# Last static expert slot of a fused attention and mixture-of-experts kernel: 32 tokens in plain fp32 and four column groups, in place of 128 tokens in split fp32r

## The chip, the core and the metric

The kernel runs on one core of one Trainium2 chip. The metric is device time in microseconds (us), the median over runs. Engines are named TensorE (PE in the profile, PEld for its weight loads), VectorE (DVE), ScalarE (ACT), GpSimd (POOL) and SyncE (SP, which issues most DMAs).

## The reference

Three layers follow each other on 2304 tokens of 512 features: a windowed attention, a dense layer pair, and a mixture of 8 experts with one expert per token. The last is what the change touches:

```python
def _moe2_ref(x, modality_id, w_gate, modality_bias, w1, w2):
    logits = x @ w_gate + modality_bias[modality_id]
    e_idx = np.argmax(logits, axis=1)
    ...
    gate_w = probs[np.arange(N), e_idx]
    for e in range(E):
        mask = e_idx == e
        ...
        h = np.maximum(x[mask] @ w1[e], 0.0)          # 512 -> 1024
        out[mask] = gate_w[mask, None] * (h @ w2[e])  # 1024 -> 512
```

Which tokens go to which expert is known only on the chip.

## The kernel before, in words

Tokens are sorted into slots of SL = 384 tokens, each slot for one expert. While the last chunk of the dense layers runs, routing tables are written: for each slot its expert, and for each place in it the token and its gate weight. Seven slots (NS0 = 7, numbered 0 to 6) are laid out in straight code; `final()` (line 729) puts the emptiest of the late slots last, and if it holds more than HS tokens it sets `nused` (line 768) so that a further full slot runs under `tc.If` (line 1227 and what follows). HS is 128 before the change (line 41).

A slot of 384 tokens (`slot`, line 851) works on TensorE in fp32r, with each operand split into a high and a low part: three matmuls (high-high, low-high, high-low) stand for one fp32 product. Layer 1 has the weights stationary, 384 tokens moving (line 858): 8 x 12 matmuls. ReLU and the split of the hidden values are ScalarE's and VectorE's (lines 860, 861). Layer 2 (`l2_slot`, line 867) goes by token tiles of 128: hidden values stationary, 512 output features moving, 24 matmuls a tile (line 873); then ScalarE scales by the gate weight (line 880) and GpSimd scatters the 128 rows to the output with an indirect DMA (line 881), where places without a token are out of bounds and are skipped.

The last slot (`half_slot`, line 887) holds one tile of 128 tokens. Layer 1 has the tokens stationary and pairs of weight blocks moving (256 columns, line 898): 4 x 12 matmuls. After ReLU (line 901) the result is turned with two transposes per pair (line 907) and split (lines 909, 910), and then the same `l2_slot` follows for one tile. Nothing of another slot is left to run beside it.

Weights of a slot come in 16 pieces of 128x512 (256 KB each, `wload`, line 783): SP loads a piece into one of four staging tiles, and three steps later ScalarE casts it to the high part and VectorE subtracts to give the low part (`wsplit`, lines 795 and 796). The tiles `experts` have two sets, for even and odd slots; slot 6 writes over slot 4's. `PS` says how many of these steps each part of a slot takes; the loads of slot 6 are issued from the sixth step of slot 4 on.

`gather` (line 816) makes a slot's list of tokens on GpSimd (three small table loads, line 820, and seven small operations) and fetches rows of 512 features (line 835). `prep_half` (line 842) turns them with four transposes a tile (line 845) and splits them. For slot 6 it stands in slot 5, in the middle of the first token tile of layer 2.

From slot 2 on TensorE's order is that of the program (a manual schedule), as is ScalarE's from the end of the dense layers, SP's throughout and GpSimd's from slot 5 on; VectorE's is chosen by the scheduler. A plain fp32 matmul shows as two records in the trace, and so does the attention's product with the values (`att_pv`, line 447), which is plain fp32 and puts two matmuls of 64 stationary columns into two column groups of the array:

```python
T.matmul(
    xo[a * D : (a + 1) * D, hp, o * BLK : (o + 1) * BLK],
    vt[:w, (2 * hp + a) * D : (2 * hp + a + 1) * D],
    ts[:w, hp, a * BLK : (a + 1) * BLK],
    start=True, stop=True,
)
```

Line 476 is plain fp32 too, a dense layer's, with all 128 stationary columns and 384 moving, four k-steps to a product.

Of the kernel before, what the change touches and what calls it, by code (L numbers as in the profile page):

```python
# [9 lines left out]
F32 = mybir.dt.float32  # L10
# [3 lines left out]
AF = mybir.ActivationFunctionType  # L14
ALU = mybir.AluOpType
AX = mybir.AxisListType

P = 128
B, H, S, D = 4, 8, 576, 64
NT = B * S  # L20
# [17 lines left out]
EARLY = 3  # L38
NS = (NT + E * (SL - 1)) // SL + EARLY
NS0 = 7  # L40
HS = P
NJ = NT // SL
NEG = -1.0e30
BIG = 1.0e6
# [2 lines left out]
def _consts():  # L47
    parts = {}
    parts["ident"] = np.eye(P)
    r = np.arange(P) % BLK  # L50
    c = np.arange(P)
    parts["m0"] = np.where(c[None, :BLK] <= r[:, None], 0.0, NEG)
    rel = (BLK + r)[:, None] - c[None, :]
    parts["m1"] = np.where((rel >= 0) & (rel < BLK), 0.0, NEG)
    parts["ones"] = np.ones((P, NS))
    parts["ids"] = np.arange(NTT)[None, :] * P + np.arange(P)[:, None] - BIG
    parts["first"] = np.broadcast_to((E - np.arange(E)).astype(float), (P, E))
    parts["eidx"] = np.broadcast_to(np.arange(E).astype(float), (P, E))
    parts["thr"] = np.broadcast_to(np.tile(np.arange(NJ) * float(SL), E), (P, NJ * E))
    parts["sidx"] = np.broadcast_to(np.arange(NS).astype(float), (P, NS))  # L60
    off, spec, arrs = 0, {}, []
    for k, a in parts.items():
        spec[k] = (off, a.shape[1])
        off += a.shape[1]
        arrs.append(np.asarray(a, np.float32))
    tri = (np.arange(P)[:, None] < np.arange(P)[None, :]).astype(np.float16)
    empty = np.zeros((NS * SL, 2), np.float32)
    return spec, np.ascontiguousarray(np.concatenate(arrs, axis=1)), tri, empty
# [3 lines left out]
def moe_kernel(ctx, tc, qT, kT, v, w_in, w_out, mod, wg, wgT, mbias, w1, w2, cst, tri, empty, out, spec):  # L72
# [17 lines left out]
    def tile_of(shape, name, dt=F32, tag=None, bufs=1):  # L90
        pool = sb if (tag or name) in WIDE else sm
        return pool.tile(shape, dt, name=name, tag=tag or name, bufs=bufs)

    def aux(shape, name):
        return ps.tile(shape, F32, name=name, tag="aux", bufs=3)
# [679 lines left out]
    GP, GN = 1, 0  # L775
    PW = KD * F2 // NP
    NLD = 3
    wld = {}

    def wpart(i, p, lo):  # L780
        return piece(i % 2, (p // NP * 2 + lo) * NP + p % NP)

    def wload(i, p):
        if p == 0:
            wld[i] = SP.value_load(
                meta[0:1, 1 if i < KNOWN else 3, i : i + 1], min_val=0, max_val=E - 1
            )
        t = tile_of([P, PW], f"wr{i}_{p}", tag=("v" if p % 2 else "q"), bufs=2)
        src = (w2 if p // NP else w1)[bass.ds(wld[i], 1), :, (p % NP) * PW : (p % NP + 1) * PW]
        SP.dma_start(t, src.rearrange("o p n -> (o p) n"))  # L790
        wld[i, p] = t

    def wsplit(i, p):
        t = wld.pop((i, p))
        A.copy(wpart(i, p, 0), t)  # L795
        V.tensor_tensor(wpart(i, p, 1), t, wpart(i, p, 0).bitcast(F32), op=ALU.subtract)  # L796

# [15 lines left out]
    def w2s(i, f, lo):  # L813
        return piece(i % 2, (2 + lo) * NP + f)

    def gather(i, rows=NT, halves=SH):
        rr = G.value_load(meta[0:1, 0 if i < KNOWN else 2, i : i + 1], min_val=0, max_val=(NS - 1) * SL)
        rt = tile_of([P, TT, SH, 2], f"rt{i}", tag="rt", bufs=2)
        for t in range(TT):
            G.dma_start(rt[:, t], tabs[t][bass.ds(rr, SL), :].rearrange("(h p) w -> p h w", p=P))  # L820
        rc = tile_of([P, SH, 2], f"rc{i}", tag="rc", bufs=4)
        oi = tile_of([P, SH], f"oi{i}", I32, tag="oi", bufs=4)
        gi = tile_of([P, SH], f"gi{i}", I32, tag="gi", bufs=4)
        gf = tile_of([P, SH], f"gf{i}", tag="gf", bufs=4)
        G.tensor_tensor(rc, rt[:, 0], rt[:, 1], op=ALU.add)
        G.tensor_tensor(rc, rc, rt[:, 2], op=ALU.add)
        G.tensor_scalar(gf, rc[:, :, 0], 0.0, None, op0=ALU.is_lt)
        G.tensor_scalar(rc[:, :, 0], rc[:, :, 0], BIG, None, op0=ALU.add)
        G.tensor_tensor(gf, gf, rc[:, :, 0], op=ALU.mult)
        G.tensor_copy(gi, gf)  # L830
        G.tensor_copy(oi, rc[:, :, 0])
        g = []
        for h in range(halves):
            t = tile_of([P, DM], f"g{i}_{h}", tag="ssk"[h], bufs=2)
            G.indirect_dma_start(t, None, yd[:rows, :], bass.IndirectOffsetOnAxis(ap=gi[:, h : h + 1], axis=0))
            g.append(t)
        return g, oi, rc

    def new_x2(i):
        return tuple(tile_of([P, KD, SL], f"z{s}{i}", F32R, tag=f"x{s}", bufs=2) for s in "hl")  # L840

    def prep_half(i, h, g, x):
        tp = aux([P, KD, P], f"tp{i}_{h}")
        for k in range(KD):
            T.transpose(tp[:, k, :], g[0][h][:, k * P : (k + 1) * P], C["ident"])
        sl = slice(h * P, (h + 1) * P)
        A.copy(x[0][:, :, sl], tp)
        V.tensor_tensor(x[1][:, :, sl], tp, x[0][:, :, sl].bitcast(F32), op=ALU.subtract)
# [17 lines left out]
    def l2_slot(i, g, t, mid, hid):  # L866
        hh, hl = hid
        yo = ps.tile([P, DM], F32, tag=f"y{t}", name=f"yo{i}_{t}", bufs=1)
        n = 0
        sl = slice(t * P, (t + 1) * P)  # L870
        for f in range(NF2):
            for a, b in ((hh, 0), (hh, 1), (hl, 0)):
                T.matmul(yo, a[f][:, sl], w2s(i, f, b), start=n == 0, stop=n == 3 * NF2 - 1)  # L873
                n += 1
            if f == NF2 // 2 - 1:
                yield
            elif f < NF2 - 1 and f % 2:
                mid()
        ob = tile_of([P, DM], f"ob{i}_{t}", tag="y", bufs=4)
        A.activation(ob, yo, AF.Copy, scale=g[2][:, t, 1:2])  # L880
        G.indirect_dma_start(  # L881
            out, bass.IndirectOffsetOnAxis(ap=g[1][:, t : t + 1], axis=0), ob, None,
            bounds_check=NT - 1, oob_is_err=False,
        )
        yield

    def half_slot(i, g, x, mid):
        hh, hl = (hm[:, u * NF2 * HS : (u + 1) * NF2 * HS].rearrange("p (f n) -> p f n", f=NF2) for u in range(2))
        xh, xl = x
        sl = slice(0, HS)  # L890

        def l1(fp):
            hp = ps.tile([P, 2, P], F32, tag="h", name=f"hp{i}_{fp}", bufs=2)
            w = [experts[i % 2, lo * NP // 2 + fp].rearrange("p (q k n) -> p k q n", q=2, k=KD) for lo in range(2)]
            n = 0
            for k in range(KD):
                for a, b in ((xh, 0), (xl, 0), (xh, 1)):
                    T.matmul(hp, a[:, k, sl], w[b][:, k], start=n == 0, stop=n == 3 * KD - 1)
                    n += 1
            r = tile_of([P, 2, P], f"hr{i}_{fp}", tag="y", bufs=4)  # L900
            A.activation(r, hp, AF.Relu)
            return r

        def turn(fp, r):
            rt = aux([P, 2, P], f"rt{i}_{fp}")
            for u in range(2):
                T.transpose(rt[:, u, :], r[:, u, :], C["ident"])
            fs = slice(2 * fp, 2 * fp + 2)
            A.copy(hh[:, fs], rt)
            V.tensor_tensor(hl[:, fs], rt, hh[:, fs].bitcast(F32), op=ALU.subtract)  # L910

        r = l1(0)
        for fp in range(1, NF2 // 2):
            yield
            r2 = l1(fp)
            turn(fp - 1, r)
            r = r2
        yield
        turn(NF2 // 2 - 1, r)
        yield from l2_slot(i, g, 0, mid, ([hh[:, f] for f in range(NF2)], [hl[:, f] for f in range(NF2)]))  # L920

    man = ExitStack()
    ET = mybir.EngineType
# [268 lines left out]
        if rts and next(rts[0], "end") == "end":  # L1192
            rts.clear()

    for i in range(NS0):
        if i == NS0 - 2:
            m2.enter_context(tc.manual_schedule(engines={ET.Pool}))
            used = nc.values_load(nused[0:1, 0:1], min_val=1, max_val=NS + 1)
        if i == 2:
            m2.enter_context(tc.manual_schedule(engines={ET.PE}))  # L1200
        nx = new_x2(i + 1) if i + 1 < NS0 else None
        for n, _ in enumerate((slot if i + 1 < NS0 else half_slot)(i, gq[i], x, advance)):
            advance()
            for _ in range(PS[n]):
                next(ws, None)
            if n == GN and EARLY <= i + GP < NS0:
                assert not rts
                gq[i + GP] = gather(i + GP, halves=SH if i + GP + 1 < NS0 else 1)
            pn = 1 if i < EARLY - 1 else NF2
            if nx is not None and pn <= n < pn + (SH if i + 2 < NS0 else 1):  # L1210
                prep_half(i + 1, n - pn, gq[i + 1], nx)
        x = nx
    m2.close()
    man.close()
# [59 lines left out]
```

## Time and profile before

| what | us |
|---|---|
| median of 3 runs | 731.57 |
| lowest and highest | 730.88 and 1313.32 |
| the profiled execution | 732.23 |
| its span, first to last instruction | 730.6 |
| TensorE busy in it | 715.6 |
| VectorE, ScalarE, GpSimd busy | 472.7, 389.9, 127.6 |

A row of a timeline reads: start in us from the span's start, duration, engine, line, operation, what it writes and reads, shapes, how many records are merged, and in brackets the engine's idle time before it with what ended it. Matmuls are pipelined: one record lasts from its issue to its last result, so records overlap, and merged records show the time that they cover together. A row by stretch gives the stretch and its length, busy us (and instructions) of PE, PEld, DVE, ACT and POOL, then the granted share of TensorE's clock, the DMA share and GB/s. A group's row gives busy us in all, mean ns of one, and the engine's idle us before them with what ended it.

### The profile page before, as it was taken

The page shows a single profiled execution, that of the slowest core. Times are in us where ns is not written, and L with a number is a line of the kernel's source. Part 1 is how long each engine was busy: PE and PEld are TensorE (multiplying, and loading weights), DVE is VectorE, ACT ScalarE, POOL GpSimd, SP SyncE. Part 2 cuts the span into 40 slices and gives each one's busy share as a digit, 9 for nine tenths or more (in the row PEclk, how much of TensorE's full clock was granted, in tenths as well). Part 3 has the DMA queues.
Part 4 walks back from the last instruction along what each step waited for, and adds up shares of the span by engine and source line. Part 5 has one row for each costly group of instructions (what it writes and reads, how often), then busy time and mean ns, then how long its engine had stood idle before and what let it go on. Part 6 is the DMA issues. An engine that isn't in the chain of part 4 may idle for free. (4 is left out here: it accounts for less than half of the span.)

```text
span 730.6 us, 12530 instructions
## 1 busy us (share of the span) xinstructions
PE 715.6 (98%) x4217; PEld 625.6 (86%) x4217; DVE 472.7 (65%) x1439; ACT 389.9 (53%) x942; POOL 127.6 (17%) x185
## 2 busy tenths in 40 slices
PE   8999999999999999999999999999999999999995
PEld 5665699888989898988998898999989989898984
DVE  4997998897497538762796548857764545453600
ACT  6788778656554536554555445545343544453511
POOL 2000200113001201120111502131058221201010
PEclk9999999999999999999999999999999999999998
DMA  9897415402231103220310015245565754444310
GB/s 321 321 340 232 173 59 195 128 20 78 87 98 44 50 15 108 74 80 16 109 59 30 2 52 165 73 88 188 161 142 175 230 175 159 160 159 158 115 42 9
DMA packets 48570, 89.26 MB, mean 122 GB/s; under 512 B 6976, under 2 KB 16320, under 8 KB 48368
## 3 DMA queue, kind: packets, MB, share of 16 engines
q1 hardware_dynamic: 44064, 78.36, 32.4%
q0 software_dynamic: 4288, 9.79, 4.7%
q8 instruction: 35, 0.57, 0.3%
q14 instruction: 39, 0.32, 0.2%
q10 hardware_dynamic: 144, 0.22, 0.1%
HBM read 78.89 MB, written 9.87 MB: 121 GB/s over the span
## 5 line engine op out<-in xcount | busy, mean ns | idle before, releaser
L497 PE MATMUL h<-xh,w 128*128 128x384 f32 x640 | 179.3, 341 | 0.0
L549 PE MATMUL py<-w,gh 128*128 128x512 f32 x522 | 161.8, 393 | 0.0
L497 PEld LDWEIGHTS h<-xh,w 128*128 128x128 f32 x640 | 117.1, 188 | 2.3
L549 PEld LDWEIGHTS py<-w,gh 128*128 128x128 f32 x522 | 96.5, 188 | 16.2
L497 PE MATMUL h<-xl,w 128*128 128x384 f32 x320 | 107.4, 336 | 0.0
L796 DVE TENSOR_TENSOR e<-wr,e 128x512 fp32r<-128x512 f32 x112 | 74.8, 690 | 46.4 <-ACT e L795 44.4
L549 PE MATMUL py<-w,gl 128*128 128x512 f32 x261 | 102.4, 396 | 0.0
L858 PE MATMUL hp<-zh,e 128*128 128x384 f32 x384 | 101.0, 336 | 0.1
L873 PE MATMUL yo<-e,hm 128*128 128x512 f32 x348 | 99.0, 394 | 0.0
L503 ACT ACTIVATE u<-h,half 128x384 f32<-128x384 f32 x96 | 55.5, 578 | 76.1 <-PE h L497 69.3
L517 DVE SCALAR_TENSOR_TENSOR u<-u,h 128x384 f32<-128x384 f32 x81 | 44.7, 552 | 68.2 <-ACT u L504 67.9
L603 DVE CUSTOM_DVE_ANT_0 prod<-y,wgb 128x512 f32<-128x512 f32 x120 | 85.9, 716 | 1.2
L529 ACT CAST gh<-u 128x384 fp32r<-128x384 f32 x81 | 41.6, 514 | 69.8 <-DVE u L517 30.7
L795 ACT CAST e<-wr 128x512 fp32r<-128x512 f32 x112 | 66.2, 616 | 18.1 <-DMA wr<-in_w 17.9
L873 PEld LDWEIGHTS yo<-e,hm 128*128 128x128 f32 x348 | 64.2, 188 | 12.4
L858 PEld LDWEIGHTS hp<-zh,e 128*128 128x128 f32 x384 | 69.7, 188 | 1.3 <-DVE hm L861 0.5
L418 POOL TENSOR_TENSOR s<-s,sm 128x512 f32<-128x512 f32 (+1 forms) x24 | 26.5, 1105 | 221.4 <-DVE sm L408 150.2
L858 PE MATMUL hp<-zl,e 128*128 128x384 f32 x192 | 64.3, 335 | 0.0
L534 DVE TENSOR_TENSOR gl<-u,gh 128x384 fp32r<-128x384 f32 x81 | 45.6, 563 | 26.0 <-ACT gh L529 24.8
L497 PEld LDWEIGHTS h<-xl,w 128*128 128x128 f32 x320 | 60.2, 188 | 1.9
L549 PEld LDWEIGHTS py<-w,gl 128*128 128x128 f32 x261 | 48.9, 188 | 10.4
L395 ACT ACTIVATE s<-s,mx 128x128 f32<-128x128 f32 (+1 forms) x120 | 45.9, 384 | 15.0 <-DVE mx L385 15.0
(218 smaller groups left out, 1048.5 us busy)
## 6 DMA issues: line engine op xcount, KB each, us to landing
wr<-in_w SPq DMA_DIRECT2D x112, 256.0 KB, 3.0
q<-in_qT SPq DMA_DIRECT2D x32, 256.0 KB, 3.3
dec<-in_w_in SPq DMA_DIRECT2D x16, 512.0 KB, 5.0
dec<-in_w_out SPq DMA_DIRECT2D x16, 512.0 KB, 4.2
v<-in_v SPq DMA_DIRECT2D x27, 256.0 KB, 3.0
k<-in_kT SPq DMA_DIRECT2D x15, 384.0 KB, 5.0
yd<-y SPq DMA_DIRECT2D x18, 256.0 KB, 2.4
wgb<-in_wgT SPq DMA_DIRECT2D x1, 2048.0 KB, 7.4
```

What stands on the lines that cost most here:

```text
L395: A.activation(s[:, hp, :n], s[:, hp, :n], AF.Exp, bias=mx[:, hp : hp + 1], scale=-1.0, accum_out=sm[:, hp : hp + 1],)
L497: T.matmul(h, wi(f, a)[:, k, :], b, start=n == 0, stop=n == 3 * KD - 1)
L503: A.activation(u, h, AF.Relu, bias=half, scale=0.5)
L517: V.scalar_tensor_tensor(g, u, 1.0, h, op0=ALU.min, op1=ALU.max)
L529: A.copy(gh, u)
L534: V.tensor_tensor(gl, u, gh.bitcast(F32), op=ALU.subtract)
L549: T.matmul(ys[c][t], a[:, sl], wo(f, b), start=f == first and n == 0, stop=f == last and n == 2)
L603: V.tensor_tensor_reduce(prod, yt[t], wgb[0][:, e, :], 1.0, 0.0, ALU.mult, ALU.add, lg[:, t, e : e + 1])
L795: A.copy(wpart(i, p, 0), t)
L796: V.tensor_tensor(wpart(i, p, 1), t, wpart(i, p, 0).bitcast(F32), op=ALU.subtract)
L858: T.matmul(hp, w1s(i, f, k, a), b[:, k, :], start=n == 0, stop=n == 3 * KD - 1)
L873: T.matmul(yo, a[f][:, sl], w2s(i, f, b), start=n == 0, stop=n == 3 * NF2 - 1)
```

## The change

HS becomes 32, and HG = 128 / 32 = 4. The last slot is no longer a stage of its own but a `mini_slot` of three steps, taken inside slot 5's layer 2. Its 32 tokens are gathered four times over (four quarters of the 128 partitions). Layer 1 is plain fp32: for each of 4 k-steps four matmuls with 32 stationary columns (the tokens), each for another 256 of the 1024 hidden features, into four quarters of the output's partitions. Layer 2 is plain fp32 too: for each of 8 k-steps four matmuls into the four quarters, one for each 128 output features. The result has 128 rows, of which row 32c + t is quarter c of token t, and the scatter addresses the output as 4 x 2304 rows of 128 features. The weights of slot 6 are loaded straight into the tiles of the even set, without staging and without a split.

```diff
-HS = P
+HS = 32
+HG = P // HS
...
+    parts["quart"] = (np.arange(P) // HS)[:, None]
...
+    ML = NS0 - 1
+    wld, minis = {}, {}
...
+        if i == ML:
+            n = p // NP * 2 * NP + p % NP
+            if n % 2 == 0:
+                minis[n // 2] = tile_of([P, 2 * WB], f"m{n // 2}", tag=parts[i % 2, n // 2][1])
+                experts.pop((i % 2, n // 2))
+            t = minis[n // 2][:, n % 2 * WB : (n % 2 + 1) * WB]
+        else:
+            t = tile_of([P, PW], f"wr{i}_{p}", tag=("v" if p % 2 else "q"), bufs=2)
...
     def wsplit(i, p):
         t = wld.pop((i, p))
+        if i == ML:
+            return
...
+            if mini:
+                src = bc(tabs[t][bass.ds(rr, HS), :], 0, HG)
+                G.dma_start(rt[:, t, 0], src)
...
+        if mini:
+            G.tensor_scalar(gf, rc[:, :, 0], float(HG), None, op0=ALU.mult)
+            G.tensor_tensor(gf, gf, C["quart"], op=ALU.add)
+            G.tensor_copy(oi, gf)
...
-    def half_slot(i, g, x, mid):
...
+    def prep_mini(i, g):
+        tp = aux([P, KD, P], f"tp{i}")
+        for k in range(KD):
+            T.transpose(tp[:, k, :], g[0][0][:, k * P : (k + 1) * P], C["ident"])
+        x = tile_of([P, KD, HS], f"z{i}", tag="xh", bufs=2)
+        A.copy(x, tp[:, :, :HS])
+        return x
+
+    def mini_slot(i, g, x):
+        hp = ps.tile([P, 2, P], F32, tag="h", name=f"hp{i}", bufs=2)
+        w = [minis[fp].rearrange("p (q k n) -> p k q n", q=2, k=KD) for fp in range(HG)]
+        rows = [slice(j * HS, (j + 1) * HS) for j in range(HG)]
+        for k in range(KD):
+            for j in range(HG):
+                T.matmul(hp[rows[j]], x[:, k, :], w[j][:, k], start=k == 0, stop=k == KD - 1)
+        r = tile_of([P, 2, P], f"hr{i}", tag="y", bufs=4)
+        A.activation(r, hp, AF.Relu)
+        yield
+        rt = aux([P, 2, P], f"rt{i}")
+        for q in range(2):
+            T.transpose(rt[:, q, :], r[:, q, :], C["ident"])
+        hid = tile_of([P, 2, P], "mini", tag="prod")
+        A.copy(hid, rt)
+        yield
+        yo = ps.tile([P, P], F32, tag="y0", name=f"yo{i}", bufs=1)
+        for f in range(NF2):
+            j, q = divmod(f, 2)
+            for c in range(HG):
+                w = minis[NP + j][:, q * WB + c * P : q * WB + (c + 1) * P]
+                T.matmul(yo[rows[c]], hid[:, q, rows[j]], w, start=f == 0, stop=f == NF2 - 1)
+        ob = tile_of([P, P], f"ob{i}", tag="y", bufs=4)
+        A.activation(ob, yo, AF.Copy, scale=g[2][:, 0, 1:2])
+        G.indirect_dma_start(
+            out.rearrange("t (c n) -> (t c) n", c=HG), bass.IndirectOffsetOnAxis(ap=g[1][:, 0:1], axis=0), ob, None,
+            bounds_check=NT * HG - 1, oob_is_err=False,
+        )
+        yield
...
-    for i in range(NS0):
+    for i in range(ML):
...
-        for n, _ in enumerate((slot if i + 1 < NS0 else half_slot)(i, gq[i], x, advance)):
+        for n, _ in enumerate(slot(i, gq[i], x, advance)):
...
+            if i + 1 == ML and n == NF2:
+                small = mini_slot(ML, gq[ML], prep_mini(ML, gq[ML]))
+            if i + 1 == ML and n > NF2 and n % 2:
+                next(small)
```

In slot 5 the steps n = 0 to 7 are layer 1, n = 9, 11 and 13 come after the first, second and third token tile of layer 2. So `prep_mini` stands where `prep_half` stood (n = 8), layer 1 of the mini slot after the first tile, its two transposes after the second, and its layer 2 after the third and last.

## Rows read from the trace of the kernel before

**Rows 1.** The page, busy time of the engines.
```profile
PE 715.6 (98%) x4217; PEld 625.6 (86%) x4217; DVE 472.7 (65%) x1439; ACT 389.9 (53%) x942; POOL 127.6 (17%) x185
```

**Rows 2.** Sums by stretch: slot 5 and the last slot.
```profile
675.50:709.00 33.50, 33.50 (x173) 30.57 (x172) 12.18 (x20) 12.20 (x23) 2.95 (x3) 1.00 0.24 79
709.00:721.80 12.80, 12.46 (x81) 10.90 (x79) 1.70 (x4) 3.39 (x9) 0.98 (x1) 1.00 0.06 23
```

**Rows 3.** Groups by line, TensorE in 641 to 709: busy, mean ns, idle.
```profile
L873 PE MATMUL yo<-e,hm 128*128 128x512 f32 x108 | 30.8, 394 | 0.0
```

**Rows 4.** Timeline of TensorE, slot 5's layer 2 and the last slot.
```profile
694.94 0.60 PE L845 MATMUL tp<-cs,g 128*128 128x128 f32 x4
...
709.01 0.28 PE L898 MATMUL hp<-e,zh 128*128 128x256 f32 x1
...
716.06 5.72 PE L873 MATMUL yo<-e,hm 128*128 128x512 f32 x24
```

**Rows 5.** The chain of waits that ended last, in order of time.
```profile
721.89 0.68 ACT ob L880
722.56 0.03 POOLq L881
...
723.32 0.99 POOL out L881
```

**Rows 6.** Timeline of GpSimd; landings of line 881 in 698:713 and in 722:731.
```profile
710.22 0.98 POOL L881 DMA_INDIRECT out<-ob,oi  x1 [4.45 <-ACT ob L880]
...
DMA to landing us min/median/max: 2.7/2.7/2.8
...
DMA to landing us min/median/max: 3.1/3.1/3.1
```

**Rows 7.** Timeline of TensorE in the early phase, plain fp32.
```profile
57.26 0.69 PE L447 MATMUL xo<-ts,v 128*64 128x64 f32 x16
57.88 2.85 PE L476 MATMUL h<-x,raw 128*128 128x384 f32 x8
...
57.88 0.59 PE L476 MATMUL h<-x,raw 128*128 128x384 f32 x1
```

**Rows 8.** Line 447: first and last records of one block; the whole group.
```profile
49.97 0.28 PE L447 MATMUL xo<-ts,v 128*64 128x64 f32 x2
...
50.42 0.23 PE L447 MATMUL xo<-ts,v 128*64 128x64 f32 x2
...
L447 PE MATMUL xo<-ts,v 128*64 128x64 f32 x432 | 16.5, 226 | 2.2 <-ACT ts L430 2.2
```

**Rows 9.** Groups by line and shape, ScalarE.
```profile
L901 ACT ACTIVATE hr<-hp 128x256 f32<-128x256 f32 x4 | 1.5, 386 | 3.8 <-PE hp L898 2.8 <-ACT hm L909 1.0
```

**Rows 10.** Timeline of GpSimd, scatters in slots 1 and 2, and their landings.
```profile
570.35 1.03 POOL L881 DMA_INDIRECT out<-ob,oi  x1 [4.41 <-ACT ob L880]
574.26 1.01 POOL L881 DMA_INDIRECT out<-ob,oi  x1 [2.88 <-DMA out<-ob,oi]
...
578.94 1.08 POOL L881 DMA_INDIRECT out<-ob,oi  x1 [1.40 <-DMA out<-ob,oi]
...
DMA to landing us min/median/max: 3.1/4.4/4.5
```

**Rows 11.** Loads of expert weights in 600 to 700 and their landings.
```profile
L790 SPq DMA_DIRECT2D wr<-in_w x41: 332/333/338, 603.3 to 687.9; - x41
...
DMA to landing us min/median/max: 2.6/2.8/3.5
```

**Rows 12.** Timeline of GpSimd, the token list of slot 6 and what follows.
```profile
610.00 0.63 POOL L829 TENSOR_TENSOR gf<-gf,rc 128x3 f32<-128x3 f32 x1
...
626.86 1.07 POOL L835 DMA_INDIRECT g<-yd,gi  x1 [15.85 <-PE tp L845]
```

**Rows 13.** Sums by stretch around three scatters, columns as in rows 2.
```profile
699.30:702.20 2.90, 2.90 (x14) 2.40 (x13) 0.00 (x0) 0.00 (x0) 0.98 (x1) 1.00 0.24 90
...
723.20:726.60 3.40, 0.00 (x0) 0.00 (x0) 0.00 (x0) 0.00 (x0) 0.99 (x1) 0.89 0.06 17
```

More of the change, by code (lines that the diff above doesn't have):

```diff
@@ L777, in moe_kernel @@
     NLD = 3
-    wld = {}
+    ML = NS0 - 1
+    wld, minis = {}, {}
     def wpart(i, p, lo):
@@ L787, in wload @@
             )
-        t = tile_of([P, PW], f"wr{i}_{p}", tag=("v" if p % 2 else "q"), bufs=2)
+        if i == ML:
[6 more added lines that the diff above has]
+            t = tile_of([P, PW], f"wr{i}_{p}", tag=("v" if p % 2 else "q"), bufs=2)
         src = (w2 if p // NP else w1)[bass.ds(wld[i], 1), :, (p % NP) * PW : (p % NP + 1) * PW]
@@ L814, in w2s, with gather @@
         return piece(i % 2, (2 + lo) * NP + f)
-    def gather(i, rows=NT, halves=SH):
+    def gather(i, rows=NT, mini=False):
+        nh = 1 if mini else SH
         rr = G.value_load(meta[0:1, 0 if i < KNOWN else 2, i : i + 1], min_val=0, max_val=(NS - 1) * SL)
@@ L819, in gather @@
         for t in range(TT):
-            G.dma_start(rt[:, t], tabs[t][bass.ds(rr, SL), :].rearrange("(h p) w -> p h w", p=P))
+            if mini:
+                src = bc(tabs[t][bass.ds(rr, HS), :], 0, HG)
+                G.dma_start(rt[:, t, 0], src)
+            else:
+                G.dma_start(rt[:, t], tabs[t][bass.ds(rr, SL), :].rearrange("(h p) w -> p h w", p=P))
         rc = tile_of([P, SH, 2], f"rc{i}", tag="rc", bufs=4)
@@ L824, in gather @@
         gf = tile_of([P, SH], f"gf{i}", tag="gf", bufs=4)
+        hs_ = slice(0, nh)
+        rt, rc, oi, gi, gf = rt[:, :, hs_], rc[:, hs_], oi[:, hs_], gi[:, hs_], gf[:, hs_]
         G.tensor_tensor(rc, rt[:, 0], rt[:, 1], op=ALU.add)
@@ L830, in gather @@
         G.tensor_copy(gi, gf)
-        G.tensor_copy(oi, rc[:, :, 0])
+        if mini:
+            G.tensor_scalar(gf, rc[:, :, 0], float(HG), None, op0=ALU.mult)
+            G.tensor_tensor(gf, gf, C["quart"], op=ALU.add)
+            G.tensor_copy(oi, gf)
+        else:
+            G.tensor_copy(oi, rc[:, :, 0])
         g = []
-        for h in range(halves):
+        for h in range(nh):
             t = tile_of([P, DM], f"g{i}_{h}", tag="ssk"[h], bufs=2)
@@ L885, in l2_slot @@
         yield
-    def half_slot(i, g, x, mid):
[L888 to L917, printed above, removed]
-        yield
-        turn(NF2 // 2 - 1, r)
-        yield from l2_slot(i, g, 0, mid, ([hh[:, f] for f in range(NF2)], [hl[:, f] for f in range(NF2)]))
@@ L1193, in advance @@
             rts.clear()
-    for i in range(NS0):
-        if i == NS0 - 2:
+    for i in range(ML):
+        if i == ML - 1:
             m2.enter_context(tc.manual_schedule(engines={ET.Pool}))
@@ L1200, in moe_kernel @@
             m2.enter_context(tc.manual_schedule(engines={ET.PE}))
-        nx = new_x2(i + 1) if i + 1 < NS0 else None
-        for n, _ in enumerate((slot if i + 1 < NS0 else half_slot)(i, gq[i], x, advance)):
+        nx = new_x2(i + 1) if i + 1 < ML else None
+        for n, _ in enumerate(slot(i, gq[i], x, advance)):
             advance()
@@ L1207, in moe_kernel @@
                 assert not rts
-                gq[i + GP] = gather(i + GP, halves=SH if i + GP + 1 < NS0 else 1)
+                gq[i + GP] = gather(i + GP, mini=i + GP == ML)
             pn = 1 if i < EARLY - 1 else NF2
-            if nx is not None and pn <= n < pn + (SH if i + 2 < NS0 else 1):
+            if i + 1 < ML and pn <= n < pn + SH:
                 prep_half(i + 1, n - pn, gq[i + 1], nx)
+            if i + 1 == ML and n == NF2:
+                small = mini_slot(ML, gq[ML], prep_mini(ML, gq[ML]))
+            if i + 1 == ML and n > NF2 and n % 2:
+                next(small)
         x = nx
```

## The prediction

> **What bounds the kernel now.** I read the page first, then the sums by stretch, then the timelines of TensorE, ScalarE and GpSimd at the end, and last the fp32 matmuls of the early phase.
>
> The page gives TensorE 98% of the span [rows 1]. By stretch [rows 2] slot 5 (675.5 to 709.0) has TensorE busy throughout at full clock, VectorE and ScalarE for 12 of 33.5 us; by line TensorE's idle time in slots 4 and 5 is 0.0 [rows 3]. So nothing that only relieves ScalarE, VectorE or the loads shortens these slots. The last slot fills 709.01 to 721.78: its first matmul starts at 709.01, and its 24 second-layer matmuls start at 716.06 and last 5.72 us [rows 4]. That is 12.77 us of TensorE, with nothing of another slot beside it. After it come 0.69 us of ScalarE (the scaled copy), 0.77 us from the copy's end to the scatter's start on GpSimd (722.56 to 723.32), and then the scatter's issue at 723.32, its landing 3.1 us later, and the closing barrier to 730.6 [rows 5, 6]. All of this is in a row. Whatever shortens 709.01 to 723.32 comes off the end one for one, until something else is late.
>
> **The change part by part.** *Removed:* the 12.77 us of TensorE and the 0.69 us copy.
>
> *Added on TensorE, layer 1:* 4 k-steps times 4 column groups, each a plain fp32 matmul with 32 stationary and 256 moving columns. The early phase shows plain fp32 [rows 7]: line 476's four k-steps leave eight records, so a matmul is two. Eight records of 384 columns take 2.85 us, one alone 0.59, so (2.85 - 0.59)/7 = 0.323 us per record; at 0.84 ns a column that is 0.217 us for 256 columns, 0.110 for 128. The same rows show column groups: line 447 has 8 matmuls in two groups of 64 columns, 16 records, and all of it lies between 57.26 and 57.88. One after the other 16 records of 64 columns would need 16 x 0.054 = 0.86 us. In the same block one round earlier the first two records fill only 0.28 us together and the last two only 0.23 [rows 8], when one alone lasts 0.23 on average: two records start together, at the first as at the last. The seven steps from 49.97 to 50.42 are 0.064 us each, where two records in a row would need 0.108. So the two groups do run side by side, at 1.7 of 2. Entering and leaving such a block costs together 0.62 - 8 x 0.054 = 0.19 us.
>
> Four groups are not in the trace of before. The bounds for layer 1: 16 x 2 x 0.217 = 6.94 us if none run side by side, 3.47 if two do, 1.73 if four do. Each group has its own columns and its own rows of the output, as the two groups of line 447 have, so I take four: 1.73 + 0.19 + 0.05 for a slow first step = 2.0 us. It stands between the first and second token tile of slot 5's second layer.
>
> *The two transposes:* (0.60 - 0.27)/3 = 0.11 us each from the four at 694.94 [rows 4]: 0.22. The four transposes of prep_mini are those that prep_half issued at the same place: no change. The waits for the copies (hidden rows, x) lie under 24 and 12 matmuls of 0.23 us ((5.72 - 0.39)/23), 5.4 and 2.7 us, against copies of 0.39 us and less [rows 4, 9].
>
> So slot 5's last token tile ends 2.2 us later than now. *Layer 2:* 8 steps x 4 groups, 128 columns: 16 x 0.110 + 0.1 = 1.9 us with four abreast (3.6 with two, 7.1 with one). TensorE then ends at 709.01 + 2.2 + 1.9 + 0.16 (what a last matmul runs over: 0.39 - 0.23 [rows 3, 4]) = 713.3. The copy of 128 columns costs about 0.24 by the line through 0.69 (512) and 0.39 (256) [rows 5, 9] and no more than the latter; with 0.09 to start it is ready at 713.6 to 713.8.
>
> *What is late next:* the scatters. All write the same output, and in the one place where they follow each other closely, the second and third waited for the landing of the one before: idle times 2.88 and 1.40 us ended by the output's DMA, issues 3.91 and 4.68 us apart [rows 10]. Before the change the last two are 13 us apart and it cannot bite. Now the scatter of slot 5's third tile moves from 710.22 to 712.42 and lands 2.7 us later [rows 6], at 715.12. GpSimd is in order, so the last scatter stands behind it, and nothing else does. From landing to issue I bound 0.3 (4.68 - 4.4) and 0.8 (3.91 - 3.1) [rows 10]; I take 0.77, the step ahead of the last scatter now, since the same branch follows it. It issues at 715.12 + 0.77 = 715.9 instead of 723.32: **7.4 us earlier.** TensorE and the copy are done 1.4 us before that landing, so layer 2's time is free up to some 3.3 us.
>
> *The last scatter itself:* 128 rows of 512 bytes instead of 2 KB. Landings here take 2.7 to 3.1 us whether a full tile or a nearly empty one is written [rows 6], once 4.4 when others were in flight [rows 10]; I keep 3.1, no gain. After it the tail is what it is now.
>
> *Costed at nothing:* 16 casts and 16 subtractions of split weights go from ScalarE and VectorE: no gain, since TensorE is busy all along [rows 2, 3]. The loads go straight into the freed weight tiles rather than through staging; a tile's load may now wait for slot 4's last read of it. Slot 4's last reads end at 675.5; the last load is issued at 687.9 now and, without staging to wait for, none has a reason to be later; it takes 2.8 us to land [rows 11], and layer 2 wants it at 711. Behind the waiting load stand on SP only slot 6's own loads. If that cover were gone, the price would be a landing, 2.8 us. The gather gains two small GpSimd operations of 0.6 us at most, where GpSimd then idles up to 15.85 us, and its three table loads get smaller [rows 12].
>
> **Sum.** The profiled execution took 732.23 us (span 730.6 and 1.6 around it): 732.23 - 7.4 = 724.8. It stands 0.66 above the median of the runs, 731.57 (one of the three, 1313.32, says nothing here), so the forecast for the median is **724.2 us**. What a measurement of this kernel tells from no change is about 2%, 14.6 us; all of slot 6 on TensorE is less than that.
>
> **The rivals.** *Two groups abreast, not four.* A fp32 matmul is two records on one group; if they are issued strictly in order, the second holds back the next group's first, and only neighbours overlap. Then layer 1 is 3.47 + 0.24, layer 2 3.5 + 0.15; slot 5 ends 3.9 us later; TensorE ends at 716.7, the copy at 717.0, the scatter issues at 717.8: 5.5 saved, **726.1 us**. For it: the trace has no four. Against it: with that order the first and the last record of line 447 would each stand alone, and both come as a pair [rows 8]. The Trainium skill's page "TensorE: Matmul & The Clock Gate" (Part 3: Packing small matmuls) states this order: matmuls start and end strictly in program order. By that rule, with a matmul's two records next to each other, this rival would hold; rows 8 agree with it only if the two groups' records are interleaved in the program. The same section has three column groups at 2.38 times one; at that worth per group, four would give an estimated 3.2 times, 2.2 us for layer 1 instead of 1.7, and 724.7 as the sum.
>
> *No waiting for the landing.* If the quarter-row view of the output is not seen as the same memory, the last scatter follows the copy: 713.7 + 0.77 = 714.5, 8.8 saved, **722.8 us**. For it: nothing in the rows but the new view. Against: rows 10.
>
> *Groups one after the other* (slower). If 32-column groups share what two 64-column groups did not have to (weight loads or the stream of moving columns), plain fp32 costs two records per matmul in full: 7.2 + 0.22 before slot 5 ends, 7.2 after it; TensorE ends at 709.01 + 14.6 + 0.16 = 723.8, the copy at 724.1, the scatter at 724.9, 1.6 later than now: **733.2 us**. It decides once layers 1 and 2 together take over about 13 us, that is, fewer than 1.1 groups abreast. Against it: line 447's 1.7.
>
> *The slot overflows.* With more than 32 tokens left for it, a further full slot runs under the branch: at least the 33.5 us of a slot [rows 2], **765 us or more**. The last scatter now moves 17 GB/s over 3.40 us, 58 KB at most with all else in that stretch, where a full one moves 261 KB [rows 13]: at most 29 rows of 2 KB. The reference with its own seed leaves 1168 - 3 x 384 = 16. So it should fit.
>
> **How the numbers follow.** Forecast 0.63 (its own range 723.0, from a landing gap of 0.3, a landing of 2.7 and no block overhead, to 725.6, where small waits for the sixteen loads' semaphores or a slower landing add a microsecond); two abreast 0.18; no wait 0.08; one after the other 0.07; overflow 0.01; 0.03 for something else late, among it the order of VectorE's and GpSimd's earlier work, which the scheduler may choose anew. The range of 722.2 to 727.2 takes in the first three with the spread of the undisturbed runs (0.7) and leaves out about 0.15. Faster by over 2% would need more than the whole slot: 0.01; slower by over 2% only the overflow or a mishap: 0.02; within 2%: 0.97.
>
> **What would show it.** Right: line 898 gone, 32 records of 128x32 with 256 columns between slot 5's first and second tile within 2.0 us, four starting together; 64 records with 128 columns in 1.9 us at the end; the last scatter's idle time ended by the output's DMA, its issue about 3.5 us after the one before it; TensorE's end 8.5 us earlier but the span only 7.4. Wrong: layer 1 taking 3.5 or 7 us; the last scatter released by ScalarE; TensorE idle in slot 5 for weights or x; any idle of TensorE before 675.

## The result: 0.9% faster, and what the profile after shows

The changed kernel takes 724.1 us (median of six runs, 723.68 to 724.56); the kernel before, run beside it, 731.0. The ratio is 0.9907 with an interval of 0.9896 to 0.9919: 0.9% faster, and within 2%. The profiled execution took 724.15 us with a span of 722.2, against 732.23 and 730.6.

The page of after, busy time of the engines and then the loads of slot 6's weights among the DMA issues (KB each, median us to landing):

```profile
PE 706.8 (98%) x4235; PEld 617.1 (85%) x4235; DVE 460.6 (64%) x1418; ACT 379.5 (53%) x920; POOL 128.7 (18%) x187
...
m<-in_w SPq DMA_DIRECT2D x16, 256.0 KB, 5.4
```

TensorE is 8.8 us less busy [rows 1], VectorE 12.1, ScalarE 10.4; only TensorE's part is seen in the time. The timeline of TensorE in after, from the transposes before slot 5's second layer to the end; L925 is slot 6's layer 1, L931 the two transposes, L940 its layer 2 [rows 4]:

```profile
693.41 0.60 PE L914 MATMUL tp<-cs,g 128*128 128x128 f32 x4
...
696.37 0.39 PE L897 MATMUL yo<-e,hl 128*128 128x512 f32 x1
696.69 1.93 PE L925 MATMUL hp<-m,z 128*32 128x256 f32 x32
698.55 2.11 PE L897 MATMUL yo<-e,hm 128*128 128x512 f32 x8
...
704.13 0.38 PE L931 MATMUL rt<-cs,hr 128*128 128x128 f32 x2
...
709.58 0.39 PE L897 MATMUL yo<-e,hl 128*128 128x512 f32 x1
709.90 1.95 PE L940 MATMUL yo<-m,mini 128*32 128x128 f32 x64
```

The same timeline, cut off just after each block has begun:

```profile
696.69 0.42 PE L925 MATMUL hp<-m,z 128*32 128x256 f32 x4
...
709.90 0.32 PE L940 MATMUL yo<-m,mini 128*32 128x128 f32 x4
```

Four records start within 0.02 us at the head of each block, and the next four of layer 1 follow 0.216 us later. Sums by stretch of slot 5 and slot 6 (columns as in rows 2):

```profile
674.00:690.64 16.64, 16.64 (x97) 16.64 (x96) 3.91 (x7) 4.14 (x8) 0.98 (x1) 1.00 0.32 112
690.64:709.90 19.26, 19.26 (x111) 14.77 (x111) 0.56 (x1) 2.79 (x6) 1.98 (x2) 1.00 0.08 29
```

TensorE has no idle time in either stretch: neither the loads of slot 6's weights nor the copies hold it up. The end, on GpSimd's timeline: slot 5's third scatter, and slot 6's.

```profile
711.02 0.99 POOL L905 DMA_INDIRECT out<-ob,oi  x1 [4.69 <-ACT ob L904]
715.45 0.98 POOL L943 DMA_INDIRECT out<-ob,oi  x1 [3.44 <-ACTq L1258]
```

And the chain of waits that ended last, from 711 on:

```profile
711.02 3.63 DMA out<-ob,oi
714.65 0.03 issue
714.68 0.04 POOLq L943
714.72 0.50 issue
715.22 0.05 POOLq L1258
715.27 0.17 issue
715.45 0.98 POOL out L943
```

Before, the chain's end ran TensorE, ScalarE's copy, scatter [rows 5]. Now it runs scatter, landing, scatter: TensorE is done at 711.85 (709.90 + 1.95). The last copy, on ScalarE's timeline:

```profile
712.62 0.37 ACT L942 ACTIVATE ob<-yo,rc 128x128 f32<-128x128 f32 x1 [1.87 <-PE yo L940]
```

It ends at 712.99, 1.66 us before the landing at 714.65. The timeline names ScalarE's branch as the releaser of the last scatter, the chain the landing of the output's DMA; the experiments decide between the two.

### The profile page after: what moved, and what is told of

It reads as the page before. It is cut to its first block, busy times and chain, and to the rows that moved or that the text cites. A ratio compares the mean times of both kernels' runs of the same rounds, so it can differ in the third digit from the quotient of the medians.

```text
span 722.2 us, 12495 instructions
## 1 busy us (share of the span) xinstructions
PE 706.8 (98%) x4235; PEld 617.1 (85%) x4235; DVE 460.6 (64%) x1418; ACT 379.5 (53%) x920; POOL 128.7 (18%) x187
## 4 chain that ended last, share of the span: by engine, by line
PE 92%; DMA 2%; ACT 2%; DVE 2%; issue 1%; SPq 0%; POOL 0%; POOLq 0%; ACTq 0%
PE h L499 25%; PE py L551 25%; PE hp L882 14%; PE yo L897 13%; PE sc L372 4%; PE xo L449 3%; PE h L478 2%; PE pt L427 2%; PE py L545 2%; PE tp L869 1%; DMA out<-ob,oi 1%; DMA lent<-in_qT 1%; DVE dt L289 1%; DVE raw L294 1%; ACT s L397 0%
## 5 line engine op out<-in xcount | busy, mean ns | idle before, releaser
L897 PE MATMUL yo<-e,hm 128*128 128x512 f32 x324 | 93.5, 395 | 0.0
L808 DVE TENSOR_TENSOR e<-wr,e 128x512 fp32r<-128x512 f32 x96 | 64.0, 690 | 34.9 <-ACT e L807 32.0
L897 PEld LDWEIGHTS yo<-e,hm 128*128 128x128 f32 x324 | 59.6, 188 | 11.8 <-issue 0.4
L807 ACT CAST e<-wr 128x512 fp32r<-128x512 f32 x96 | 56.7, 618 | 16.9 <-DMA wr<-in_w 16.8
L551 PEld LDWEIGHTS py<-w,gl 128*128 128x128 f32 x261 | 48.9, 188 | 10.4
```

The source lines that it names most:

```text
L551: T.matmul(ys[c][t], a[:, sl], wo(f, b), start=f == first and n == 0, stop=f == last and n == 2)
```

## The experiments

Two theories stood against each other for the last 10 us. *Landing:* the end is set by the last scatter, which waits for the landing of the scatter before it; TensorE and the copy have room. *TensorE:* the end is set by TensorE's last matmul, and the scatter follows its copy. Beside them stands the question how the four column groups came to cost 4 us and not 14.

A number that doesn't depend on how the run began is the time from the issue of slot 5's first scatter to the issue of the last one of all. It is 23.98 us in the kernel before, profiled again, and 17.58 in the changed kernel, profiled again (17.64 in the first profile). TensorE's last end in the table is counted from the span's start and does depend on it: slot 5's first matmul starts anywhere between 673.80 and 674.71 in the changed kernel and its variants.

| kernel | median us | ratio to before, interval | TensorE's last end | last issue after slot 5's first |
|---|---|---|---|---|
| before, again | 730.52 (one execution) | | 720.56 | 23.98 |
| changed, again | 724.4 | 0.9915, 0.9902 to 0.9928 | 712.08 | 17.58 |
| own stage | 722.62 | 0.9886, 0.9872 to 0.9901 | 713.64 | 16.44 |
| slot 6 inside layer 1 | 722.2 | 0.988, 0.9866 to 0.9894 | 713.19 | other order |
| layer 2 one tile earlier | 721.69 | 0.9873, 0.9859 to 0.9887 | 712.52 | 15.31 |
| the same, again | 721.44 | 0.9876, 0.9858 to 0.9894 | 711.90 | 15.32 |
| the same, last copy in halves | 722.17 | 0.9882, 0.9864 to 0.9899 | 712.02 | 15.68 |
| table of its own | 721.46 | 0.987, 0.9853 to 0.9886 | 712.25 | 15.38 |
| layer 2 in pairs | 723.83 | 0.9906, 0.9889 to 0.9922 | 713.50 | 17.11 |
| one group after the other | 728.82 | 0.9975, 0.9963 to 0.9987 | 718.97 | 22.02 |
| 128 rows, no groups | 731.8 | 1.0011, 1.0002 to 1.0021 | 722.65 | 25.68 |
| overflow | 782.24 (one execution) | | 768.51 | other order |

**Both kernels once more.** No edit.

> The changed kernel once more, as the base of this group: 723.7 to 724.5 us. Both theories: the same. The landing theory (the end is set by the last scatter, which waits for the landing of the one before) wants the last scatter's idle time ended by the output's DMA again, some 0.8 us after that landing. The TensorE theory (the end simply follows the last matmul, and the wait for the landing was a chance of one execution) wants it released by ScalarE in another execution.

> The kernel before once more, one look. The profiled execution of before took 732.23 us, over 1 us more than most of its runs, and TensorE was already 1.2 us later there after the first ten microseconds. If that was a chance of the first loads, this look takes 730.7 to 731.2 us and its last slot starts at the time that the changed kernel's numbers imply (about 707.5 to 708); if the change itself brought 1.2 us at the start, this look shows the late start again and takes about 732.

Measured 724.4, as expected, and 730.52, a little under the range of 730.7 to 731.2; its last slot starts at 707.79, as expected. The timeline of the changed kernel names ScalarE's branch ahead of the last scatter again, so it does not give the sign that was asked for; the end of the chain is the same as in the first profile:

```profile
711.25 3.57 DMA out<-ob,oi
...
715.61 0.98 POOL out L943
```

**Slot 6 after slot 5 instead of inside it.** Its steps run behind slot 5's last tile.

```diff
-            if i + 1 == ML and n > NF2 and n % 2:
-                next(small)
         x = nx
+    for _ in small:
+        pass
```

> The mini slot is not taken inside slot 5 but after it: layer 1, ReLU, transposes, copy, layer 2 in a row, with two pauses of TensorE of about 0.7 us each. Landing theory: slot 5's last scatter is issued 2.3 us earlier and has landed before the mini slot is done, so the two pauses cost less than the wait that goes: about 0.7 us less, 723.4 us. TensorE theory: two pauses more, 725.5 us.

Measured 722.62, 0.8 below the landing theory's 723.4. The work on TensorE is the same and ends 1.0 us *later* than in the changed kernel, counted from slot 5's first matmul (38.93 against 37.90 us), since the transposes and layer 2 now wait for ScalarE's copies, 0.55 and 0.46 us; timeline of TensorE:

```profile
708.30 1.93 PE L925 MATMUL hp<-m,z 128*32 128x256 f32 x32
...
710.79 0.44 PE L931 MATMUL rt<-cs,hr 128*128 128x128 f32 x2 [0.55 <-ACT hr L927]
...
711.69 1.95 PE L940 MATMUL yo<-m,mini 128*32 128x128 f32 x64 [0.46 <-ACT mini L933]
```

Yet the last scatter is issued 1.1 us earlier (16.44 against 17.58): slot 5's third scatter is issued at 709.42 and has landed at 712.15, 2.07 us before the last copy is ready:

```profile
714.98 0.98 POOL L943 DMA_INDIRECT out<-ob,oi  x1 [4.58 <-ACT ob L942]
```

By the TensorE theory this kernel is slower than the changed one. It falls here.

**Layer 2 one tile earlier.** Slot 6's layer 1 stays behind slot 5's first token tile, its transposes go into the middle of the second tile, and its layer 2 follows the second tile, so that the small scatter comes before slot 5's last one.

```diff
-            if i + 1 == ML and n > NF2 and n % 2:
+            if i + 1 == ML and n in (NF2 + 1, NF2 + 2, NF2 + 3):
```

> The mini slot's three steps stand half a token tile apart, so its layer 2 and its scatter come before slot 5's third token tile instead of after it. TensorE has the same work. Landing theory: the last scatter is then slot 5's third tile; the mini slot's scatter has 5.4 us of TensorE to land in; from TensorE's end 0.7 us of copy and 0.8 to issue: about 2.1 us less, 721.8 to 722.4 us. TensorE theory: the same end of TensorE and a copy 0.3 us longer: 724.4 us.

> The same order with the whole copy on ScalarE, for the comparison on the same chip: 721.4 to 722.0 us.

721.69 and 721.44; the first is 2.7 us below the changed kernel beside it and 0.1 below the range. GpSimd's timeline, then ScalarE's:

```profile
709.55 0.98 POOL L943 DMA_INDIRECT out<-ob,oi  x1 [2.55 <-DMA out<-ob,oi]
713.56 0.98 POOL L905 DMA_INDIRECT out<-ob,oi  x1 [3.03 <-ACT ob L904]
...
712.60 0.69 ACT L904 ACTIVATE ob<-yo,rc 128x512 f32<-128x512 f32 x1 [5.18 <-PEq L1258]
```

The wait for a landing is still there, but it now falls on the small scatter, which nothing follows closely; the last one is released by its copy again. TensorE has as much to do as before the edit. Part of the gain is something else: from the copy's end (713.29) to the scatter's start are 0.27 us, where the kernel before and the changed one need 0.77 and 0.80 from what releases them [rows 5]. In the chains of those two, 0.5 us of issue stand between the release and the branch that GpSimd takes next (714.72 to 715.22 in after); here the branch follows the copy at 713.33. No run moved this part alone.

**Slot 6 inside slot 5's layer 1.**

```diff
-            if i + 1 == ML and n == NF2:
+            if i + 1 == ML and n == 1:
                 small = mini_slot(ML, gq[ML], prep_mini(ML, gq[ML]))
-            if i + 1 == ML and n > NF2 and n % 2:
+            if i + 1 == ML and n in (3, 5, 7):
                 next(small)
```

(Layer 1's sums move to another PSUM tag as well.)

> The whole mini slot stands inside slot 5's layer 1 (its scatter is issued some 20 us before the end), with its layer-1 result in another accumulator bank. Landing theory: no scatter is near another one, the last is released by ScalarE, and the end follows TensorE's: 721.4 to 722.2 us, no slower than the version before it. TensorE theory: 724.4 us. If the weights come too late at this earlier place, TensorE idles in slot 5's layer 1 and the time is 724 or more.

722.2. All scatters are released by copies, and slot 5's are some 5.5 us apart:

```profile
708.80 0.98 POOL L905 DMA_INDIRECT out<-ob,oi  x1 [4.46 <-ACT ob L904]
714.25 0.98 POOL L905 DMA_INDIRECT out<-ob,oi  x1 [4.46 <-ACT ob L904]
```

So it gains for the landing theory's reason. TensorE ends 0.7 us later here than with layer 2 one tile earlier, because it stands idle once, before slot 5's first token tile:

```profile
696.55 2.12 PE L897 MATMUL yo<-e,hm 128*128 128x512 f32 x8 [0.62 <-ACT ob L942]
```

That tile and slot 6's layer 2 use the same PSUM tag, and the tile waits for ScalarE's copy of slot 6's result.

**A table of its own for the small scatter.** Slot 6's rows go to a scratch table in DRAM, so they are missing from the output; the transfer, the matmuls and their order stay.

```diff
-            out.rearrange("t (c n) -> (t c) n", c=HG), bass.IndirectOffsetOnAxis(ap=g[1][:, 0:1], axis=0), ob, None,
+            spare[:, :], bass.IndirectOffsetOnAxis(ap=g[1][:, 0:1], axis=0), ob, None,
```

> The mini slot's scatter writes to a table of its own instead of the output (the last slot's rows are so left out of the output); it need not wait for another landing. Landing theory: it is issued 0.8 us after its copy, 1.5 to 2 us earlier; it lands before slot 5's last scatter has been followed by anything, so the end moves by about 1.5 us: 722.4 us. TensorE theory: no change, 724.1 us.

721.46, 0.9 below the landing theory's forecast. This is the plainest test: only the target differs, and the last scatter goes out 2.17 us after the third although that one lands only at 715.25:

```profile
711.42 0.98 POOL L906 DMA_INDIRECT out<-ob,oi  x1 [4.69 <-ACT ob L905]
713.59 0.98 POOL L944 DMA_INDIRECT spare<-ob,oi  x1 [1.19 <-ACT ob L943]
```

The wait for the landing is there because both write the same output, and it costs the changed kernel 2.2 us at the issue (17.58 - 15.38), 2.4 in the spans of the two profiled executions (722.5 and 720.1) and 2.9 in the medians; what makes the medians differ by more was not found.

**Layer 2 in pairs.** The same 64 records, with only two column groups next to each other in the program.

```diff
-        for f in range(NF2):
+        for f, c in ((f, 2 * h + u) for h in range(2) for f in range(NF2) for u in range(2)):
```

> Layer 2 of the mini slot alone goes two column groups at a time: 3.6 us instead of 1.95. Landing theory: TensorE ends 1.7 us later, which the wait for slot 5's last scatter covers (the copy was ready 2.4 us before the last scatter's issue): 724.0 us, no change within 0.4. TensorE theory: 1.7 us more, 725.8 us.

723.83, no loss, though the block is 1.34 us longer and TensorE's end, counted from slot 5's first matmul, 1.33 later:

```profile
710.21 3.29 PE L939 MATMUL yo<-m,mini 128*32 128x128 f32 x64
```

Its last scatter's wait is named by the landing outright:

```profile
715.23 0.98 POOL L942 DMA_INDIRECT out<-ob,oi  x1 [2.91 <-DMA out<-ob,oi]
```

That landing took 3.10 us, against 3.57 and 3.63 in the changed kernel, so the last issue is even earlier (17.11 against 17.58). The changed kernel has at least 1.3 us of room on TensorE: a slower layer 2 costs nothing up to here, and a faster one should bring nothing. (The block was expected to take 3.6 us; the next experiment shows why it takes less.)

**One group after the other.** In both layers the loop over groups goes outside.

```diff
-        for k in range(KD):
-            for j in range(HG):
+        for j in range(HG):
+            for k in range(KD):
...
-        for f in range(NF2):
+        for c, f in ((c, f) for c in range(HG) for f in range(NF2)):
```

> The order of the mini slot's matmuls is changed so that all steps of one column group follow each other: nothing can run side by side. Theory of the four groups abreast: layer 1 takes 32 x 0.217 = 6.9 us instead of 1.9 and layer 2 64 x 0.110 = 7.0 instead of 1.95; TensorE ends 10 us later, the wait for the landing no longer matters, the end moves by 10.1 - 2.7 of cover = about 7.5: 731.5 us, no faster than the kernel before. Rival (the gain is that of plain fp32 and the smaller tile, groups matter little): 724 to 726 us.

728.82: the landing theory's 731.5 was missed by 2.7 us. The two blocks in its chain of waits:

```profile
697.21 4.52 PE hp L925 x32
...
713.09 5.90 PE yo L939 x64
```

They were expected to need 7 us each. The timeline of TensorE, cut at 698.02 and at 698.04, says why:

```profile
697.14 1.05 PE L925 MATMUL hp<-m,z 128*32 128x256 f32 x4
...
697.14 1.30 PE L925 MATMUL hp<-m,z 128*32 128x256 f32 x6
```

Four records start alone, 0.22 us apart (the first step 0.24); the fifth and the sixth start together, at 698.025 and 698.031. Two records of one group never do so (in the kernel with 128 rows below, all 32 of layer 1 follow each other at 0.216 us). The sixth lasts 0.403 us like the first of the block, where the others last 0.379. So I read it as the next group's first, with three of the first group's eight still to come. The next change, at 698.918 and 698.924, is the same. So the groups begin 0.894 us apart, and layer 1 is 3 x 0.894 + 8 x 0.216 + 0.16 = 4.57 us, as measured (4.59 in the timeline). In layer 2 the next group begins with the thirteenth record of 16, three left again: 3 x 1.34 + 16 x 0.109 + 0.16 = 5.92 (5.95 in the timeline). In layer 2 in pairs, above, the second pair's first records start at 711.559, right behind the thirteenth ones of the first pair (711.547 and 711.554), again with three left. So TensorE doesn't hold strictly to the program's order across column groups. The Trainium skill's page "TensorE: Matmul & The Clock Gate" (Part 3: Packing small matmuls) says that it does, in start and end; for the starts of this kernel's column groups the trace shows otherwise.

**128 rows, no groups.** Slot 6 again holds 128 rows, with plain fp32, unsplit loads and the place inside slot 5 kept from the change; the main lines:

```diff
-HS = 32
-HG = P // HS
+HS = P
+HG = 4
...
+            T.matmul(yo, hid[:, f], minis[NP + j][:, q * WB : (q + 1) * WB], start=f == 0, stop=f == NF2 - 1)
```

> The change without its column groups: the last slot holds 128 tokens again, in plain fp32 with all 128 stationary columns, its weights loaded unsplit, and its steps inside slot 5 as in the changed kernel. TensorE by the rows of plain fp32: layer 1 16 x 2 x 0.217 = 6.9 us instead of 1.9, eight transposes instead of two (0.7 more), layer 2 8 x 2 x 0.43 = 6.9 instead of 1.95. Theory of the four groups: TensorE ends 10.6 us later, the wait for the landing is covered, the end moves by about 8.5 us: 732 us, no faster than before. Rival (what brought the gain is the missing split and the place inside slot 5): 726 us or less.

731.8 (1.0011): nothing gained. Its chain of waits, layer 1 and layer 2:

```profile
697.09 6.91 PE hp L919 x32
...
715.78 6.88 PE yo L932 x16
```

13.8 us of matmuls in place of the 12.77 that the whole last slot took on TensorE in the kernel before [rows 2, 4]. Plain fp32, the unsplit loads and the place inside slot 5 bring nothing alone. The matmuls here move as many columns as the changed kernel's, 32 x 256 and 16 x 512 (there 64 x 128), so its shorter blocks come from the groups side by side. The 32 rows by themselves also save six transposes, priced at 0.7 us above; 32 rows without any overlap were not run. 6.91 against 1.93 us for the same 32 records is 3.6 times.

**Overflow.** The threshold is set so that slot 6's tokens no longer fit and a further full slot runs under the branch.

```diff
-        V.tensor_scalar(big, big, float(NS * (SL - HS)), None, op0=ALU.is_lt)
+        V.tensor_scalar(big, big, float(NS * (SL - 8)), None, op0=ALU.is_lt)
```

> The threshold of the last slot is lowered to 8 tokens, while it still can hold 32: its 16 tokens are then too many, and the further full slot runs under its branch. Prices what a remainder over 32 costs the changed kernel. Nothing hides its gather, its 16 weight loads and its own stage: the 33.5 us of a slot on TensorE, less the little that overlaps, and 15 to 40 us of loads and splits ahead of it: 724 + 50 to 75 = 774 to 800 us.

782.24 in one execution. TensorE waits 15.5 us for the further slot's rows and comes back at a granted clock of 0.50, that is 1.2 GHz; timeline and sums by stretch:

```profile
727.45 1.08 PE L869 MATMUL tp<-cs,g 128*128 128x128 f32 x4 [15.49 <-DMA g<-yd,gi]
...
720.00:730.00 10.00, 2.15 (x8) 1.43 (x8) 2.50 (x5) 2.32 (x5) 5.15 (x10) 0.50 0.62 188
```

**The last copy in halves**, on top of layer 2 one tile earlier: the first 256 columns on ScalarE, the rest on VectorE.

```diff
+            A.activation(ob[:, :dh], yo[:, :dh], AF.Copy, scale=g[2][:, t, 1:2])
+            V.tensor_scalar(ob[:, dh:], yo[:, dh:], g[2][:, t, 1:2], None, op0=ALU.mult)
```

> The order with the mini slot's layer 2 before slot 5's last token tile, and that tile's scaled copy split in halves over ScalarE and VectorE: 0.39 instead of 0.69 us at the end. Landing theory (there the last scatter is released by the copy, not by a landing): 0.3 us less, 721.4 us. If the last scatter there waits for something else, no change: 721.7 us.

722.17, 0.7 us slower than the same order with the whole copy on ScalarE (721.44): the halves ran one after the other, 1.04 us in all instead of 0.69. ScalarE's and VectorE's timelines:

```profile
712.11 0.47 ACT L906 ACTIVATE ob<-yo,rc 128x256 f32<-128x256 f32 x1 [5.18 <-PEq L1263]
...
712.67 0.48 DVE L907 TENSOR_SCALAR ob<-yo,rc 128x256 f32<-128x256 f32 x1 [20.83 <-ACT ob L906]
```

VectorE's half waits for ScalarE's. Whether the shared source or the shared target orders them was not tried.

The version that beats both kernels is thus the one with layer 2 one tile earlier: 721.4 to 721.7 us, some 9 us under the kernel before.

## Why the prediction was right, and where one term was not

The forecast was 724.2, the measurement 724.1 and 724.4. The mechanism held, but the hit owes something to two errors that cancel.

- **Four column groups abreast: right.** The quads at the head of both blocks show it. Layer 1 was put at 2.0 us. The block starts 0.32 us after the last 512-column matmul instead of 0.23, the next tile's first follows 1.86 later, and that tile's first eight records need 2.11 where eight in a row of before need 1.98: 0.09 + 1.86 + 0.13 = 2.1. Layer 2 was put at 1.9 and 0.16 of overrun, and shows 1.95 with the overrun in it. From the transposes at 693.41 to TensorE's end it is 18.44 us; the prediction's sum, 709.01 + 2.2 + 1.9 + 0.16 - 694.94 [rows 4], is 18.33.
- **Costed at nothing: right.** No idle time of TensorE in slot 5. The unsplit loads take 5.4 us to land instead of 2.8 [rows 11], but the last is issued at 674.7, some 13 us sooner than before, and the cover held. GpSimd's longer token list ends at 610.0, and its next work is at 625.3 [rows 12].
- **The scatters are late next: right,** and shown by the table of its own, the own stage and the pairs. The step from landing to issue was put at 0.77 and is 0.80.
- **The landing of slot 5's third scatter: too short.** The step "lands 2.7 us later" measured 3.63, and 3.57 in the second profile. With slot 5's last tile 0.1 later than forecast this makes the saving at the last issue 23.98 - 17.58 = 6.4 us where the sum says 7.4.
- **The starting point: too high.** The sum began from a median of 731.57; the kernel before measured 731.0 with the result and 730.59, 730.51 and 731.05 beside the later runs. Its profiled execution had lost about 1.1 us in the first 10 us of the program (TensorE's seventeenth first-stage matmul began at 9.70 us, at 8.61 in the second profile), which the stretch around the change doesn't contain. A base 0.5 to 1.1 too high and a saving 1.0 too large gave a time that fits.
- **The tail after the last issue** was taken as unchanged. It was 7.3 us in the profile that the forecast used, 6.7 in the same kernel's second profile, and 6.8 and 6.9 in the two of the changed kernel: no effect of the change is to be seen beside what executions differ by.
- **The copy of 128 columns** was put at 0.24 and no more than 0.39, and took 0.37: it lay under the wait. The line was drawn through two different operations, a scaled copy of 512 columns and a ReLU of 256 [rows 5, 9]. The scaled copy of 256 columns takes 0.47 (the copy in halves), and 0.37, 0.47 and 0.69 do lie on a line, some 0.26 us and 0.84 ns a column.
- **Small slips in the sum.** At 0.84 ns a column 256 columns are 0.215 us and 128 are 0.108, not 0.217 and 0.110; the changed kernel shows 0.216 and 0.109. Over both layers this is about 0.05 us.

Of the rivals, *no waiting* forecast 722.8: the table of its own is that rival made real, at 721.46, and the changed kernel is not it. *Two abreast* fell with the quads; its reason, strict order, fell with the single groups. By the Trainium skill's page "TensorE: Matmul & The Clock Gate" (Part 3: Packing small matmuls) the estimate for four groups was 3.2 times one; the runs have 3.6. *One after the other* forecast 733.2; the kernel with 128 rows, whose matmuls do run one after the other, took 731.8. *Overflow* was bounded at 765 or more and came to 782, as the bound left out the wait for the rows and the slower clock after it.

**Why the landing was 3.6 and not 2.7** is seen but not tested. The queues' view of after between 711 and 714.7, and of the own stage between 709.4 and 712.2 (packets, MB, share of 16 engines):

```profile
q0 software_dynamic: 80, 0.26, 19.2%
q8 instruction: 1, 0.02, 1.5%
q14 instruction: 1, 0.01, 0.6%
```

```profile
q0 software_dynamic: 80, 0.26, 24.4%
issues: line engine op xcount, KB each, median us to landing
out<-ob,oi POOLq DMA_INDIRECT x1, 2.7
```

The same 80 packets, but in after an instruction packet lies among them: 1.5% of 16 engines over 3.7 us is 0.9 us of one engine. Over the profiles of this study, a full tile's scatter of slot 5 took 3.2 to 3.8 us to land where such a packet started 0.5 to 1.3 us after its issue (twelve times), 2.7 to 3.1 where it started 2.4 us after or later (three times), and 2.7 to 2.8 without one (once 3.0). That the one makes the other long fits by size and place; no run moved the packet alone.

## What to carry to other kernels

When a tail is shortened, follow the in-order queue of its last write: a scatter that writes the same tensor waits for the landing of the one before it, here 2.7 to 3.6 us and 0.8 to the next issue, and two scatters closer than some 4 us make that wait the new end. A small job that was put inside a large one should therefore hand in its result before the large one's last, not after; that was worth 2.7 us here, for one changed line. Where a duration decides the forecast, take it from several instances and not from the one in the right place: the rows on hand had landings of 2.7, 3.1 and 4.4 us.

## What the hardware did that was not expected

- Records of different column groups overlap even when the program runs the groups one after the other: the next group's first starts while three of the former's are still to come. That cut 7 us to 4.59 in layer 1 and to 5.95 in layer 2.
- On ScalarE the kind of operation counts as much as the columns: a scaled copy of 256 columns (the scale is a column of the tile `rc`) took 0.47 us, a ReLU of as many 0.39 and a plain copy 0.37; a scaled copy of 128 columns took 0.37 and a plain one 0.27.
- After 15.5 us without matmuls TensorE came back at a granted clock of 0.50 (the overflow run).
